# A fused attention and mixer kernel: what its planner counts of the DMA queue, when a batch's first sum is turned, and where the last 64 keys' scores come from

## The chip, the cores and the metric

The kernel runs on one core of one Trainium2 chip. The metric is device time in microseconds (us) of one execution. Of the kernel before there are three timed executions and one profiled execution. TensorE (PE) does the matmuls, VectorE (DVE) and ScalarE (ACT) the elementwise work, GpSimd (POOL) a few casts at the start, and SyncE (SP) issues every DMA, one after the other, in the order in which the program has them.

## The reference

There are 8 batches; a sequence has S = 3136 rows, D = 256, the attention's inner size is 64, the mixer's rank is 32 and its hidden size is 1024.

```
scores = z @ z.T / S                    # (3136, 3136), symmetric
attn   = max(scores, 0) ** 2
x      = u * (attn @ v)                 # (3136, 256)
h      = x.T @ U @ V                    # rank 32, along the sequence
u2     = x + h.T
out    = u2 + max(u2 @ w_ch1, 0) @ w_ch2
```

All inputs and the output are float32 in memory. The kernel casts to bfloat16 for the matmuls and accumulates in float32. S is 24 full tiles of 128 rows and a tail of 64 rows.

## The kernel before

**Tiling.** A batch's rows form groups: six of 512 rows (g = 0 to 5, four tiles each) and one of 64 rows (g = 6). An "item" is one pair (batch b, group g); the main loop runs over the 56 items in order and emits the matmuls of an item's attention times v ("AV"), interleaved with scores that later items need and with mixer work of items that lie a batch back. Nearly all matmuls use 64 of the 128 rows of the array and go in pairs, one pair member on each half of the rows (`pair`, L159); so line L164 is the line of nearly every matmul.

**Scores.** The scores of a batch are made by key block J and query group g into "blocks" (128 x 4 x 512 bf16, L383): matmuls of 512 columns into PSUM, `rectify` (L317) out of PSUM by ACT or DVE, `square` (L313) by DVE. Scores are symmetric. Most blocks with J > g are therefore made once, and the block for (b, J, g) is the transpose of the block for (b, g, J): `issue_turn` (L336) takes a free block and issues a transposing DMA on SP. There are 20 blocks; `take_block` and `give_block` pass them around.

**The last 64 keys.** The tail's keys against the 512 queries of a group are a job called "last", one for each two groups, three a batch (`jobs_of`, L906; L355 and L378): a pair of matmuls of 512 columns, a rectify and a square into `last_sb`. `av_end` (L599) reads it as the last step of a group's AV. The tail's 64 queries against all keys are made apart by `score_small` (L416) into `attn_small`, which is read by `av_small` (L552), the AV of group 6. By symmetry `attn_small` holds the same numbers as the "last" scores, turned.

**The mixer.** `t1_all` (L630) makes x.T @ U for a whole batch once all seven groups have x. `u2_unit` (L661) makes h for a group by matmuls, DVE adds x to it (L708, `out_sb`, float32), `cast` (L181) makes the bf16 copy into `x_bf` on whichever of ACT and DVE the planner holds to be free sooner, and `x_turn` (L621) turns that copy by a DMA into `u2T`. `ch1_part` (L753) multiplies w_ch1 with `u2T`, so its first matmul of a group has to wait for that DMA; `ch2_stream` (L795) does w_ch2, and `ch2_out` (L823) adds and stores.

**What sets the order.** The program is emitted by a planner in Python that keeps a clock in its own units (L96, one unit is a matmul pair of 256 columns: `pe`, L121) and three estimates in `free_at`: when ACT, DVE and the SP queue will be free. `book` (L102) adds a cost to one of them, `hold` (L106) defers an action to a time, and `run_held` (L109) does what is due after each emitted piece. A block that is squared becomes ready to be turned (`ready_turns`); `run_held` issues one when the estimate for SP says that the queue is free (L118), each turn being booked at 34 units (L345). Loads, stores and the turns of z and x are not booked. If AV comes to a block that has not been turned, `lhs` in `av_stream` (L509) issues the turn at that place. `emit` (L857) merges three queues of work into the stream of AV and ch2 matmuls by places that are written out in the main loop. Engines and the DMA queue each run their own instructions in program order; waits between them are semaphores.

Of the kernel before, what the change touches and what calls it, by code (L numbers as in the profile page):

```python
# [9 lines left out]
BF16 = mybir.dt.bfloat16  # L10
# [8 lines left out]
def kernel(  # L19
# [17 lines left out]
    P = 128  # L37
# [60 lines left out]
    held = []  # L98
    unturned = {}
    ready_turns = []  # L100

    def book(eng, ready, cost):  # L102
        free_at[eng] = max(free_at[eng], ready) + cost
        return free_at[eng]

    def hold(due, f):  # L106
        held.append((due, len(held), f))

    def run_held(now=None):  # L109
        now = clock[0] if now is None else now  # L110
        while True:
            ripe = [h for h in held if h[0] <= now]
            if not ripe:
                break
            h = min(ripe, key=lambda e: (e[0], e[1]))
            held.remove(h)
            h[2]()
        while ready_turns and free_at["sp"] <= now:  # L118
            issue_turn(min(ready_turns, key=lambda e: (e[0], e[2], e[1])))

    def pe(cost):  # L121
# [75 lines left out]
    def load_tail(raw, c0, a, n):  # L197

        for h in range(2):
            nc.sync.dma_start(out=raw[h * TAIL : (h + 1) * TAIL, c0 : c0 + n], in_=a[NF * P : S, :])  # L200


    def load_z_piece(b, t0, n, raw, tail=True):
        m = min(n, NF - t0)
        nc.sync.dma_start(  # L205
            out=raw[:, : m * dqk].rearrange("p (t d) -> p t d", d=dqk), in_=rows_of(z[b])[:, t0 : t0 + m, :]
        )
        if n > m and tail:
            load_tail(raw, m * dqk, z[b], dqk)
            load_tail(raw, n * dqk, v[b], D)  # L210
# [15 lines left out]
    def load_v_piece(b, k, raw):  # L226
        nc.sync.dma_start(
            out=raw.rearrange("p (t d) -> p t d", d=D), in_=rows_of(v[b])[:, k * GT : (k + 1) * GT, :]
        )

    def v_copy(b, k, raw, copy):
        copy(out=v_bfs[b][:, k * GT : (k + 1) * GT, :], in_=raw.rearrange("p (t d) -> p t d", d=D))
# [41 lines left out]
    def load_u(b, g):  # L274
        g0, gw = groups[g]
        t = pool.tile([P, GT, D], FP32, name="u_sb", bufs=2)
        if gw >= P:
            nc.sync.dma_start(
                out=t[:, : gw // P, :],
                in_=rows_of(u[b])[:, g0 // P : (g0 + gw) // P, :],  # L280
            )
        else:
            nc.sync.dma_start(out=t[:gw, 0, :], in_=u[b, g0 : g0 + gw, :])
        u_sbs[b, g] = t


    def z_turn_dma(b):
        nc.sync.dma_start_transpose(
            out=zzTs[b], in_=z_bfs[b].rearrange("p t c d -> p (t c d)")
        )  # L290

    def z_turn(b, t0, copy):
        n = min(2 * GT, NT - t0)
# [55 lines left out]
    def score_pairs(jobs):  # L349

        made = []
        for b, g, job in jobs:
# [23 lines left out]
                GW,  # L376
            )
            if job == "last":  # L378
                lasts[b, g // 2] = pool.tile([P, 2, GW], BF16, name="last_sb")
                made.append((lasts[b, g // 2], k, ps, None, None))  # L380
                continue
            if h == 0:
# [30 lines left out]
        score_finish(score_pairs(jobs))  # L413


    def score_small(b, g):  # L416
        zzT = zzTs[b]
        g0, gw = groups[g]
# [5 lines left out]
        for p0 in range(0, npair, per):  # L424
            n = min(per, npair - p0)
            pk, ps = take_ps()
            for k in range(n):
                pair(
                    pk,
                    [  # L430
                        (
                            jj,
                            jj,
                            dict(
                                out=ps[:, jj, k * gw : (k + 1) * gw],
                                lhsT=half(zzT, jj, (2 * (p0 + k) + jj) * P, P),
                                rhs=half(zzT, jj, g0, gw),
                                start=(k == 0),
                                stop=(k == n - 1 and (jj == 1 or p0 + n < npair)),
                            ),  # L440
                        )
                        for jj in range(2)
                    ],
                    gw,
                )
            made.append((p0, n, pk, ps))
# [105 lines left out]
    def av_small(b, g):  # L552
# [3 lines left out]
        for jt in range(NT):  # L556
            c = jt % 2
            for h in range(2):
                nc.tensor.matmul(  # L559
                    out=ps[c * hp : c * hp + rows, h, :D],  # L560
                    lhsT=smalls[b][h * hp : (h + 1) * hp, jt, :],
                    rhs=v_bfs[b][h * hp : (h + 1) * hp, jt, :],
                    start=(jt < 2),
                    stop=(jt >= NT - 2),
                    tile_position=(h * hp, c * hp),
                )
# [31 lines left out]

    def av_end(b, g, box):  # L599

        last = lasts[b, g // 2]
        for a in range(2):
            pair(
                box["k"],
# [2 lines left out]
                    a,  # L607
                    lambda h, q: dict(
                        out=four(box["ps"])[:, q, :],
                        lhsT=last[h, g % 2, q * P : (q + 1) * P],  # L610
                        rhs=v_bfs[b][h, NF, :],
                        start=False,
                        stop=(a == 1),
# [7 lines left out]
    def x_turn(b, g, turned):  # L621
# [3 lines left out]
            out=turned[:, :n, :, :rows].rearrange("p q d c -> p (q d) c"),  # L625
            in_=xs[b, g][:rows, :n, :].rearrange("p q d -> p (q d)"),
        )


    def t1_all(b):  # L630
# [30 lines left out]
    def u2_unit(b, g, turn=True):  # L661
# [161 lines left out]
    def ch2_out(b, g, acc):  # L823
# [6 lines left out]
        nc.vector.tensor_tensor(out=o, in0=acc, in1=o, op=ALU.add)  # L830
        dst = rows_of(out[b])[:, t0 : t0 + n, :] if rows == P else out[b, t0 * P : S, None, :]
        nc.sync.dma_start(out=dst, in_=o)
        if (b, g) in o_blocks:
            give_block(o_blocks.pop((b, g)))

# [80 lines left out]
    def load_U():  # L916
        entry, raw = stage_block()
        nc.sync.dma_start(out=raw[:, : NF * R].rearrange("p (t r) -> p t r", r=R), in_=rows_of(moe_U))
        nc.sync.dma_start(out=raw[:TAIL, NF * R : NT * R], in_=moe_U[NF * P :, :])

        def casts():
            cast(U_bf[:, :NF, :], raw[:, : NF * R].rearrange("p (t r) -> p t r", r=R), NF * R)
# [5 lines left out]
    def load_w(k):  # L928
        def step(i):
# [4 lines left out]
            else:  # L934
# [2 lines left out]
                    in_=moe_w_ch2.rearrange("(t p) d -> p t d", p=P)[:, i * GT : (i + 1) * GT, :],  # L937
                )
                dst = w2_bf[:, i * GT : (i + 1) * GT, :].rearrange("p t d -> p (t d)")

            def casts(entry=entry, raw=raw, dst=dst):
                cast(dst, raw, GT * D)
# [7 lines left out]
    def load_V(i0):  # L950
        n = P // 4

        def step(i):
            entry, raw = stage_block()
            w = n * NF + (S - NF * P if i == 3 else 0)
            for c in range(NREP):
                nc.sync.dma_start(out=raw[c * R : (c + 1) * R, :w], in_=moe_V[:, i * n * NF : i * n * NF + w])

            def casts(i=i, entry=entry, raw=raw):
                cast(  # L960
# [102 lines left out]
    for b in range(B):  # L1063
        for g in range(NQ):
# [18 lines left out]
    for t in range(n_items):  # L1083
# [169 lines left out]
```

## Time and profile before

| what | us |
|---|---|
| three timed executions | 1010.28, 1007.97, 1010.57 |
| their median | 1010.28 |
| the profiled execution's own time | 1010.08 |
| its span, from the first to the last instruction | 1008.3 |
| TensorE matmul busy in the span | 986.7 (98%) |
| VectorE busy | 653.6 (65%) |
| ScalarE busy | 520.2 (52%) |
| DMA queue q1, share of the 16 DMA engines' span | 76.3% |

The span is cut by engine: a busy time is the time in which the engine ran at least one instruction. TensorE matmuls overlap in pairs, so the mean duration of one matmul is longer than the time by which it pushes the next. The profile's row of granted clock says what share of TensorE's full speed the chip gave it in a slice. A wait in the profile has the form "who waited <- for whom: total, times, longest"; a row of the timeline has start, duration, engine, line, operation, output<-input, count, and in brackets the idle time before it with what ended it. SPq rows are DMA issues on SP: their duration is the time that the queue was occupied with the issue, and the data lands later.

### The profile page before, as it was taken

How to read it: one execution, taken by the hardware profiler on the slowest of the kernel's cores; microseconds unless marked ns; L12 is line 12 of the kernel's file. 1: busy time of each engine (PE TensorE's matmuls, PEld its weight loads, DVE VectorE, ACT ScalarE, POOL GpSimd, SP SyncE). 2: the span in 40 equal slices, each digit the busy share in tenths (PEclk: the TensorE clock that was granted, in tenths of full speed). 3: DMA queues.
4: the chain of work that ended last, by engine and by line, in shares of the span. 5: the costliest groups of instructions: out<-in, count | busy, mean ns of one | idle time of the engine just before them, and what ended most of it. 6: DMA issues, size and time to landing. Idle time of an engine off the chain costs nothing.

```text
span 1008.3 us, 35337 instructions
## 1 busy us (share of the span) xinstructions
PE 986.7 (98%) x16179; PEld 784.7 (78%) x16179; DVE 653.6 (65%) x820; ACT 520.2 (52%) x599; POOL 17.2 (2%) x24
## 2 busy tenths in 40 slices
PE   6999899999999999999999999999999999999997
PEld 3898688877787777778777877778777777787776
DVE  5986675668666685666756677566776667653453
ACT  6896653357524573355733456444653356522453
POOL 4100000000000000000000000000000000000000
PEclk9999899999999999999999999999999999999999
DMA  7997998478966799568995789846798577873142
GB/s 247 187 257 178 235 170 166 130 166 186 213 142 165 152 199 218 149 145 181 182 209 157 129 193 188 210 127 140 179 216 185 137 158 143 160 127 88 45 103 94
DMA packets 337061, 167.84 MB, mean 166 GB/s; under 512 B 312336, under 2 KB 315408, under 8 KB 336912
## 3 DMA queue, kind: packets, MB, share of 16 engines
q1 hardware_dynamic: 336912, 165.59, 76.3%
q8 instruction: 126, 2.06, 0.8%
q14 instruction: 23, 0.19, 0.1%
HBM read 62.56 MB, written 25.69 MB: 88 GB/s over the span
## 4 chain that ended last, share of the span: by engine, by line
PE 94%; DVE 2%; ACT 2%; DMA 1%; issue 0%; POOL 0%; SPq 0%; POOLq 0%; ACTq 0%
PE ps L164 92%; PE ps L559 1%; DVE blk L315 1%; ACT blk L793 1%; PE ps L635 1%; DMA blk<-in_v_dram 1%; ACT blk L325 1%; PE ps L843 0%; DMA u2T<-x_bf 0%; DMA stage<-in_v_dram 0%; POOL z_bf L213 0%; SPq L205 0%; DVE blk L321 0%; DVE out_sb L708 0%; DVE blk L830 0%
## 5 line engine op out<-in xcount | busy, mean ns | idle before, releaser
L164 PEld LDWEIGHTS <-blk 64*128 64x128 bf16 x12288 | 617.6, 94 | 153.6 <-POOLq L154 8.7
L164 PE MATMUL ps<-v_bf,blk 64*128 64x256 bf16 x9216 | 617.2, 270 | 2.3 <-DVE blk L315 1.8
L325 ACT ACTIVATE blk<-ps 128x1024 bf16<-128x1024 f32 x324 | 323.4, 1027 | 337.2 <-PE ps L164 334.0
L315 DVE TENSOR_TENSOR blk<-blk 128x1024 bf16<-128x1024 bf16 x352 | 237.7, 701 | 34.1 <-ACT blk L325 33.4
L164 PE MATMUL ps<-u2T,w_bf 64*128 64x512 bf16 (+1 forms) x1792 | 239.1, 351 | 4.3 <-DMA u2T<-x_bf 3.5
L164 PE MATMUL ps<-w_bf,blk 64*128 64x256 bf16 x3072 | 193.7, 269 | 0.2
L790 DVE TENSOR_SCALAR blk<-ps 128x1024 bf16<-128x1024 f32 x96 | 115.7, 1205 | 102.3 <-PE ps L164 102.3
L793 ACT ACTIVATE blk<-ps 128x1024 bf16<-128x1024 f32 (+1 forms) x128 | 107.3, 847 | 82.4 <-PE ps L164 74.1
L164 PE MATMUL ps<-zzT 64*128 64x512 bf16 (+1 forms) x944 | 143.5, 342 | 1.9 <-ACT zzT L305 1.7
L164 PEld LDWEIGHTS <-w_bf 64*128 64x128 bf16 x1792 | 91.6, 94 | 35.1 <-DMA u2T<-x_bf 3.8
L592 DVE TENSOR_TENSOR x_bf<-ps,u_sb 128x1024 bf16<-128x1024 f32 x48 | 58.8, 1224 | 63.0 <-PE ps L164 62.9
L708 DVE TENSOR_TENSOR out_sb<-ps,x_bf 128x1024 f32<-128x1024 f32 (+1 forms) x49 | 54.3, 1107 | 53.7 <-PE ps L164 53.6
L830 DVE TENSOR_TENSOR out_sb<-ps,out_sb 128x1024 f32<-128x1024 f32 x42 | 51.3, 1222 | 18.3 <-PE ps L164 18.3
L164 PEld LDWEIGHTS <-zzT 64*128 64x128 bf16 x944 | 43.9, 95 | 9.2 <-ACT zzT L305 2.2
L325 ACT ACTIVATE last_sb<-ps 128x1024 bf16<-128x1024 f32 x23 | 23.5, 1024 | 26.5 <-PE ps L164 26.5
L321 DVE TENSOR_SCALAR blk<-ps 128x1024 bf16<-128x1024 f32 x24 | 29.4, 1224 | 10.3 <-PE ps L164 8.7
L186 DVE CAST x_bf<-out_sb 128x1024 bf16<-128x1024 f32 x33 | 22.8, 690 | 0.5
L186 DVE CAST v_bf<-stage 128x1024 bf16<-128x1024 f32 (+1 forms) x34 | 21.2, 626 | 0.0
L164 PE MATMUL ps<-t_sb,V_bf 64*128 64x256 bf16 x200 | 20.8, 269 | 0.0
L164 PE MATMUL ps<-v_bf,last_sb 64*128 64x256 bf16 x192 | 18.6, 269 | 0.0
L830 DVE TENSOR_TENSOR blk<-ps,blk 128x1024 f32<-128x1024 f32 x6 | 7.3, 1225 | 16.0 <-PE ps L164 15.9
L578 ACT COPY u_sb<-ps 64x512 f32<-64x512 f32 x8 | 4.7, 582 | 23.9 <-PE ps L559 23.9
(67 smaller groups left out, 249.5 us busy)
## 6 DMA issues: line engine op xcount, KB each, us to landing
u_sb<-in_u_dram SPq DMA_DIRECT2D x48, 512.0 KB, 5.0
stage<-in_v_dram SPq DMA_DIRECT2D x42, 512.0 KB, 6.0
out_dram<-out_sb SPq DMA_DIRECT2D x42, 512.0 KB, 3.1
stage<-in_z_dram SPq DMA_DIRECT2D x7, 512.0 KB, 5.5
blk<-in_v_dram SPq DMA_DIRECT2D x6, 512.0 KB, 7.2
out_dram<-blk SPq DMA_DIRECT2D x6, 512.0 KB, 2.6
blk<-in_moe_w_ch_dram SPq DMA_DIRECT2D x4, 512.0 KB, 5.8
stage<-in_z_dram SPq DMA_DIRECT2D x7, 256.0 KB, 5.7
```

Of the source, the lines that this page charges most:

```text
L164: ins = nc.tensor.matmul(**args)
L186: nc.vector.tensor_copy(out=out, in_=in_)
L315: nc.vector.tensor_tensor(out=a, in0=a, in1=a, op=ALU.mult)
L321: nc.vector.tensor_scalar(out=dst, in0=src, scalar1=scale, scalar2=0.0, op0=ALU.mult, op1=ALU.max)
L325: nc.scalar.activation(out=dst, in_=src, func=AF.Relu, scale=scale)
L559: nc.tensor.matmul(out=ps[c * hp : c * hp + rows, h, :D], lhsT=smalls[b][h * hp : (h + 1) * hp, jt, :], rhs=v_bfs[b][h * hp : (h + 1) * hp ...
L592: nc.vector.tensor_tensor(out=xs[b, g][:rows, :n, :], in0=four(box["ps"])[:rows, :n, :], in1=u_sbs[b, g][:rows, :n, :], op=ALU.mult,)
L635: nc.tensor.matmul(out=pt[c * R : (c + 1) * R, 0, :D], lhsT=U_bf[:rows, it, :], rhs=xs[b, g][:rows, q, :], start=(it < NREP), stop=(it + N ...
L708: nc.vector.tensor_tensor(out=o[:rows, :n, :], in0=four(ps)[:rows, :n, :], in1=x, op=ALU.add)
L790: nc.vector.tensor_single_scalar(out=r, in_=ps[:, :, :gw], scalar=0.0, op=ALU.max)
L793: nc.scalar.activation(out=r, in_=ps[:, :, :gw], func=AF.Relu)
L830: nc.vector.tensor_tensor(out=o, in0=acc, in1=o, op=ALU.add)
```

## The change

The change has three parts.

First, a new helper `queued` books the SP estimate for every transfer: plain ones by their size, turning ones (z and x) at about twice that rate. `run_held` therefore holds the turns of score blocks back for as long as the estimate says that loads and stores occupy the queue.

Second, for a batch's first group (g = 0) `u2_unit` is placed earlier in its item (place 22 in place of 34), its bf16 copy is emitted on DVE right behind the add, its `x_turn` is held until six units before the copy's booked end, and while it is pending (`urgent`) no turn of a score block is issued by `run_held`.

Third, for batches 1 to 7 there are no "last" jobs. `last_turn` turns the first 24 tiles of `attn_small` (1536 columns, 12 tiles of 128 columns) with one transposing DMA into `last_sb`, at the start of the batch's first item. For that `score_small` of the next batch is emitted in item g = 5 of the batch before it (batch 0's own in item g = 4), the tiles of `attn_small` are kept in a swapped order (`place_of`), and `last_sb` has one buffer in place of two, so that batch 0's "last" jobs for g = 2 and g = 4 move one item later.

```diff
+    urgent = []
...
+    def queued(kb, turned=False):
+
+        book("sp", clock[0], kb * (17 / 256 if turned else 15 / 512))
...
-        while ready_turns and free_at["sp"] <= now:
+        while ready_turns and free_at["sp"] <= now and not urgent:
             issue_turn(min(ready_turns, key=lambda e: (e[0], e[2], e[1])))
...
         for h in range(2):
             nc.sync.dma_start(out=raw[h * TAIL : (h + 1) * TAIL, c0 : c0 + n], in_=a[NF * P : S, :])
+            queued(n / 4)
...
             out=zzTs[b], in_=z_bfs[b].rearrange("p t c d -> p (t c d)")
         )
+        queued(NT * P / 4, True)
...
             if job == "last":
-                lasts[b, g // 2] = pool.tile([P, 2, GW], BF16, name="last_sb")
+                flat = last_tile().rearrange("p n c -> p (n c)")
+                lasts[b, g // 2] = flat[:, : 2 * GW].rearrange("p (a c) -> p a c", c=GW)
...
+    def place_of(jt):
+
+        if jt == NF:
+            return jt
+        return jt // GT * GT + (0, 2, 1, 3)[jt % GT]
+
+    def last_tile():
+        return pool.tile([P, NF // 2, P], BF16, name="last_sb", bufs=1)
+
+    def last_turn(b):
+
+        lasts[b] = last_tile()
+        nc.sync.dma_start_transpose(
+            out=lasts[b], in_=smalls[b][:, :NF, :].rearrange("p t c -> p (t c)")
+        )
+        book("sp", clock[0], 26)
...
-        last = lasts[b, g // 2]
+        def last(h, q):
+            if b:
+                return lasts[b][h, 2 * g + q % 2, :]
+            return lasts[b, g // 2][h, g % 2, q * P : (q + 1) * P]
...
             x_turn(b, g, u2Ts[b, g])
+            urgent.clear()
...
-        hold(done - 3, down)
+        if g == 0:
+            urgent.append((b, g))
+            nc.vector.tensor_copy(out=x, in_=o[:rows, :n, :])
+            hold(book("dve", done, 6.3) - 6, turned)
+        else:
+            hold(done - 3, down)
...
-        if g % 2 == 0:
+        if g % 2 == 0 and b == 0:
             j.append((b, g, "last"))
...
+            elif b == 0 and g and g % 2 == 0:
+                todo[t] += new[:-1]
+                todo[t + 1] += new[-1:]
...
+        if g_now == 0 and t:
+            last_turn(att[0])
...
-        if av and g_now == NQ - 1:
-            qm.append((55, 2, False, lambda: score_small(att[0], NQ)))
+        if av and t == NQ - 2:
+            qm.append((55, 2, False, lambda: score_small(0, NQ)))
+        if av and g_now == NQ - 1 and b_next < B:
+            qm.append((55, 2, False, lambda: score_small(b_next, NQ)))
...
-            qm.append((34 if u2i[1] == 0 else 40, 1, False, lambda: u2_unit(*u2i)))
+            qm.append((22 if u2i[1] == 0 else 40, 1, False, lambda: u2_unit(*u2i)))
```

More of the change, by code (lines that the diff above doesn't have):

```diff
@@ L207, in load_z_piece @@
         )
+        queued(m * dqk / 2)
         if n > m and tail:
@@ L229, in load_v_piece @@
         )
+        queued(GT * D / 2)
     def v_copy(b, k, raw, copy):
@@ L283, in load_u @@
             nc.sync.dma_start(out=t[:gw, 0, :], in_=u[b, g0 : g0 + gw, :])
+        queued(gw)
         u_sbs[b, g] = t
@@ L435, in score_small @@
                                 out=ps[:, jj, k * gw : (k + 1) * gw],
-                                lhsT=half(zzT, jj, (2 * (p0 + k) + jj) * P, P),
+                                lhsT=half(zzT, jj, place_of(2 * (p0 + k) + jj) * P, P),
                                 rhs=half(zzT, jj, g0, gw),
@@ L560, in av_small @@
                     out=ps[c * hp : c * hp + rows, h, :D],
-                    lhsT=smalls[b][h * hp : (h + 1) * hp, jt, :],
+                    lhsT=smalls[b][h * hp : (h + 1) * hp, place_of(jt), :],
                     rhs=v_bfs[b][h * hp : (h + 1) * hp, jt, :],
@@ L609, in av_end @@
                         out=four(box["ps"])[:, q, :],
-                        lhsT=last[h, g % 2, q * P : (q + 1) * P],
+                        lhsT=last(h, q),
                         rhs=v_bfs[b][h, NF, :],
@@ L627, in x_turn @@
         )
+        queued(n * D / 4, True)
     def t1_all(b):
@@ L832, in ch2_out @@
         nc.sync.dma_start(out=dst, in_=o)
+        queued(n * rows)
         if (b, g) in o_blocks:
@@ L919, in load_U @@
         nc.sync.dma_start(out=raw[:TAIL, NF * R : NT * R], in_=moe_U[NF * P :, :])
+        queued(NF * R / 2)
         def casts():
@@ L939, in step @@
                 dst = w2_bf[:, i * GT : (i + 1) * GT, :].rearrange("p t d -> p (t d)")
+            queued(GT * D / 2)
             def casts(entry=entry, raw=raw, dst=dst):
@@ L957, in step @@
                 nc.sync.dma_start(out=raw[c * R : (c + 1) * R, :w], in_=moe_V[:, i * n * NF : i * n * NF + w])
+                queued(w / 8)
             def casts(i=i, entry=entry, raw=raw):
```

## The prediction

> **What bounds the kernel now.** I read the page first, then the stretches by batch, then who TensorE waited for, then the timeline at the places that these named.
>
> ```profile
> span 1008.3 us, 35337 instructions
> ...
> PE 986.7 (98%) x16179; PEld 784.7 (78%) x16179; DVE 653.6 (65%) x820; ACT 520.2 (52%) x599; POOL 17.2 (2%) x24
> ...
> PEclk9999899999999999999999999999999999999999
> ...
> PE 94%; DVE 2%; ACT 2%; DMA 1%; issue 0%; POOL 0%; SPq 0%; POOLq 0%; ACTq 0%
> ```
>
> TensorE is busy for 98% of the span and carries 94% of the chain that ended last. So a matmul taken away shortens the time, and work taken from DVE or ACT does so only where TensorE stands still for it. Table of stretches (start:end, length, busy time of each engine with count, then granted clock, DMA share, GB/s):
>
> ```profile
> core 0: us, PE busy (x) PEld busy (x) DVE busy (x) ACT busy (x) POOL busy (x), PEclk, DMA share, GB/s
> 92.25:118.34 26.09, 22.07 (x398) 17.80 (x393) 18.33 (x28) 17.00 (x22) 0.00 (x0) 0.98 1.10 220
> ...
> 114.84:118.38 3.54, 0.00 (x1) 0.00 (x0) 1.42 (x2) 0.00 (x0) 0.00 (x0) 0.88 1.23 168
> 118.34:130.40 12.06, 11.78 (x131) 7.53 (x132) 6.11 (x8) 7.45 (x9) 0.00 (x0) 0.75 1.02 203
> 330.42:452.08 121.66, 121.57 (x2019) 95.69 (x2017) 81.24 (x103) 60.87 (x72) 0.00 (x0) 1.00 0.83 173
> 452.08:573.74 121.66, 121.57 (x2019) 95.62 (x2017) 81.22 (x103) 60.87 (x72) 0.00 (x0) 1.00 0.88 173
> 938.72:1008.30 69.58, 63.91 (x998) 48.60 (x993) 33.71 (x40) 30.42 (x38) 0.00 (x0) 1.00 0.30 84
> ```
>
> A middle batch takes 121.66 us with TensorE busy for 121.57 of it: there only matmuls can be saved. One place differs: 3.54 us without a matmul, and behind it 12.06 us at 0.75 of the clock, the one dip in the row PEclk. What was waited for:
>
> ```profile
> PE ps L164 <- DMA u2T<-x_bf: 3.5, 1, 3.5
> ```
>
> ```profile
> 105.05 0.38 PE L164 MATMUL ps<-t_sb,V_bf 64*128 64x256 bf16 x4
> ...
> 105.47 1.22 DVE L708 TENSOR_TENSOR out_sb<-ps,x_bf 128x1024 f32<-128x1024 f32 x1
> 106.61 1.28 DVE L315 TENSOR_TENSOR blk<-blk 128x1024 bf16<-128x1024 bf16 x2
> ...
> 107.81 0.69 DVE L186 CAST x_bf<-out_sb 128x1024 bf16<-128x1024 f32 x1
> ...
> 109.22 4.64 SPq L341 DMA_TRANSPOSE blk<-blk  x1
> ...
> 113.96 1.25 SPq L624 DMA_TRANSPOSE u2T<-x_bf  x1
> ...
> 114.22 0.62 PE L164 MATMUL ps<-v_bf,blk 64*128 64x256 bf16 x8
> ...
> 118.38 1.04 PE L164 MATMUL ps<-u2T,w_bf 64*128 64x512 bf16 x4 [3.54 <-DMA u2T<-x_bf]
> ```
>
> The first mixer group's x + h is in bf16 at 108.5, but SP spends 109.22 to 113.86 on the turn of a score block; only then is x turned, and it lands 4.4 us later, at the matmul's start. This place costs 3.54 us of standing and 12.06 x (1 - 0.75) = 3.0 us of clock: 6.5 us.
>
> The sums below start from the profiled execution's own 1010.08 us (its span plus 1.8 us around it), 0.2 under the median 1010.28. About 0.3%, 3 us, is what a measurement of this kernel can tell from no change.
>
> **The change, part by part.**
>
> **1. The "last" scores of batches 1 to 7 go: 21 jobs.** Each is a pair of matmuls of 512 columns, an eviction and a square.
>
> ```profile
> 332.19 0.40 PE L164 MATMUL ps<-zzT 64*128 64x512 bf16 x2
> ...
> 332.41 1.39 PE L164 MATMUL ps<-v_bf,blk 64*128 64x256 bf16 x22
> ```
>
> ```profile
> L325 ACT ACTIVATE last_sb<-ps 128x1024 bf16<-128x1024 f32 x23 | 23.5, 1024 | 26.5 <-PE ps L164 26.5
> L315 DVE TENSOR_TENSOR last_sb<-last_sb 128x1024 bf16<-128x1024 bf16 x24 | 16.4, 683 | 0.2 <-ACT last_sb L325 0.2
> ```
>
> Such a pair moves the next matmul by 332.41 - 332.19 = 0.22 us; 21 of them are 4.6 us, all on TensorE's path: -4.6. The evictions (21 x 1.02 us on ACT) and squares (21 x 0.68 us on DVE) lie beside the matmuls, and cost nothing to lose except at one place of each batch, item g = 6, where the last job of the next batch's g = 0 stands among w_ch1 matmuls:
>
> ```profile
> 341.51 1.02 ACT L793 ACTIVATE blk<-ps 128x1024 bf16<-128x1024 f32 x1
> ...
> 342.09 0.40 PE L164 MATMUL ps<-zzT 64*128 64x512 bf16 x2
> ...
> 342.54 1.02 ACT L325 ACTIVATE last_sb<-ps 128x1024 bf16<-128x1024 f32 x1
> ```
>
> By the spacing above a matmul should follow that pair at 342.31; the next one starts when the eviction by L793 has ended, at 342.58, so TensorE loses 0.27 us. In the changed order the same w_ch1 matmuls take PSUM tiles that were emptied earlier. Six batches have this pattern: between 0 (another eviction is as late) and -1.6; I take -1.6, as the two tiles in question are asked for over 1 us after their evictions can start.
>
> **2. last_turn: 7 transposing DMAs, of 12 tiles each.** No row shows one. The turns around it do:
>
> ```profile
> blk<-blk SPq DMA_TRANSPOSE x112, 5.2
> u2T<-x_bf SPq DMA_TRANSPOSE x55, 3.3
> ```
>
> A block turn has 16 tiles, an x turn 8, so about 4.2 us from issue to landing and some 2 us of the queue. The first reader is `av_end` of group 0, some 15 us of matmuls later: 0. It has TensorE's last reads of the single `last_sb` buffer to wait for, which lie an item back. What stands behind it on SP is z's load for the next batch (read 16 us later) and the first x_turn, see 4. `score_small` is as often there as before, one batch earlier: 0. `place_of` only permutes: 0.
>
> **3. The first x + h sooner (batch 0's mixer, the wait at 114.84).** In the changed order `u2_unit` stands 1.0 us of matmul columns earlier, the copy follows the add with no squares between (0 in place of 1.2 us), and on SP the block turn of 109.22 is behind it; in front are last_turn, z's loads and two loads of u, all but the first of which had gone out before 109.22 in the kernel before. So: add about 104.5 to 106, copy to about 107, turn issued by then, landed within 4.4 us, 111.4. The reader comes at about 114.5. Wait and dip go: -6.5. What is late next here is nothing that I can find; 3 us of cover remain. If they were used up by the DMA engines, which are full in this stretch (share 1.10 over 92.25 to 118.34), the -6.5 shrinks to 0 (rival two).
>
> **4. Loads and stores are booked: block turns are held back.** This moves DMAs, and adds none. In batches 0 and 1, where the weights are loaded too, the estimate for SP now runs ahead of the planner's clock for long, and turns wait until AV needs them. I counted in both programs how much matmul work stands between what a DMA waits for and its first reader. For block turns the least was 27 us of columns; now it is 19, with one exception of 4.0. That is batch 1, the turn of the block for g = 4, J = 5, needed by AV of group 5. AV found it not turned and issued it at the place of use, so it stands on SP right behind an x_turn that has only just become possible:
>
> ```
> L351 DmaTransposeAnt blk19_3981<-blk9_3864
> L656 DmaTransposeAnt u2T_4046<-x_bf_1650
> L351 DmaTransposeAnt blk0_4058<-blk10_3230      # the late one
> ```
>
> The first two stand in the same order in the kernel before, and TensorE's matmuls there are the same too (16 of AV, 2 scores, 4 of w_ch1, 14 of AV, the small scores, 16 of AV, 4 of w_ch1, 2 of AV, then the reader), so the rows of before give the times:
>
> ```profile
> 203.69 6.28 SPq L341 DMA_TRANSPOSE blk<-blk  x2
> ...
> 205.71 0.40 PE L164 MATMUL ps<-t_sb,V_bf 64*128 64x256 bf16 x4
> ...
> 207.89 0.69 DVE L186 CAST x_bf<-out_sb 128x1024 bf16<-128x1024 f32 x1
> ...
> 209.89 0.82 PE L164 MATMUL ps<-v_bf,blk 64*128 64x256 bf16 x12
> 210.05 1.69 SPq L624 DMA_TRANSPOSE u2T<-x_bf  x1
> ```
>
> ```profile
> blk<-blk SPq DMA_TRANSPOSE x3, 4.4
> ```
>
> SP is free of the x_turn at 210.05 + 1.69 = 211.74, the block's turn goes out at 211.75, and lands 4.4 us later (the median of the three between 195 and 220 us): 216.1. The reader would start two matmuls into the row at 209.89, at 210.0. TensorE stands still for 6.1 us, between 5.7 (the x_turn occupies SP for 1.25 us, as in the row at 113.96) and 7.0 (landing in 5.2, the median of all block turns). Nothing else can run meanwhile: TensorE's queue is in order, and behind the reader are all the rest of AV, scores and mixer. A wait of 3.54 us was followed by a dip that cost 3.0 us; I take 3.0 for this longer one too, between 0 (no dip) and 3.0. Together +9.1, between +5.7 and +10.0.
>
> [...]
>
> In the middle batches the x_turns come no later relative to their readers: in the changed order the first group's has 9.2 us of columns (7.1 before), the third's stands ahead of the block turn that it followed, and the others are within 0.5. 0, and small gains are not to be had where TensorE is busy throughout.
>
> **5. The end.** The tail (938.72 on, TensorE idle for 5.7 us of 69.58) has the same order but for names: 0.
>
> **Sum:** 1010.08 - 4.6 - 1.6 - 6.5 + 9.1 = 1006.5 us.
>
> **The rivals.**
>
> One: the block's turn is not late, because SP runs ahead of what I think. Against it: the x_turn in front of it needs the copy that ends at 208.58 and occupies SP for 1.25 us at least, and with 4.4 us to landing the data cannot be there before 214.2, against 210.0. For it: only that I read the order of a program and not a run. 1010.08 - 4.6 - 1.6 - 6.5 = 997.4 us.
>
> Two, the slower side: the first x_turn is late all the same, with last_turn in the place of the block turn. The place is SP at 100 to 107 us; for it speak the DMA share of 1.10 there, and that a block turn in that stretch occupied the queue for 4.64 us. It decides if the turn of x lands later than about 114.5, that is, goes out after 110. If last_turn only takes the place of the block turn, the 6.5 us stay, 1013.0; if it comes on top of the same loads and the turn of x goes out 1 us later than the 113.96 of before, 4.5 + 3.0 us are lost here: 1006.5 + 7.5 = 1014.0, the price I give it.
>
> Three: the booking changes nothing that matters and last_turn's load on the DMA engines (share 0.83 in a middle batch) makes x_turns late in each batch. Price from the dip and a wait of 1 us: 6 batches x 1 us and two dips, 1006.5 + 12 = 1018. Against it: 12 tiles come to some 315 a batch (15 block turns of 16, six x turns of 8, the turn of z of 25), 4%.
>
> **How the numbers follow.** Forecast 0.66, rival one 0.15, rival two 0.12, rival three 0.07. The forecast's own range is 1003 to 1009 (the ends of the wait, the dip and of part 1). For 8 in 10 the range reaches from rival one, 997, up to 1012.5, short of rival two as priced; what is left out is rivals two and three. Faster by over 0.3% means under 1007.2: six tenths of the forecast's cases and all of rival one, 0.55. Within 0.3%: the rest of the forecast and some of rival two, 0.31. Slower: 0.14.
>
> **What would show it.** Right: TensorE's waits have no x_turn at 115 us, and have one wait for a block's turn of about 6 us near 200 us; PEclk dips there and not at 118; a middle batch takes 120.7 us in place of 121.66; zzT matmuls of 512 columns are 42 fewer; seven new turns of 12 tiles land in about 4 us. Wrong: no wait near 200 us (then 997), a wait at 115 us (then 1013), waits that come back in each batch (then 1018), or a middle batch still at 121.66.

## The result and the profile after

The changed kernel takes 1005.4 us (median of 5 runs, 1003.74 to 1007.66); the kernel before, run beside it, 1010.57 us (1007.97 to 1011.47). The ratio is 0.9956, with a 95% interval of 0.9937 to 0.9976: 0.44% faster, 1.1 us under the forecast of 1006.5 and inside its range. The profiled execution took 1006.67 us, with a span of 1004.8.

From the page of the changed kernel, its span, busy times and granted clock in 40 slices:

```profile
span 1004.8 us, 35249 instructions
...
PE 980.5 (98%) x16137; PEld 781.4 (78%) x16137; DVE 635.6 (63%) x793; ACT 505.9 (50%) x584; POOL 17.2 (2%) x24
...
PEclk9999999989999999999999999999999999999999
```

There are 42 matmuls fewer, and the one dip of the clock (6.83 us at 0.50 of full speed: 207.44 to 214.27, before 117.52 to 124.35) has moved from the fifth slice to the ninth. What TensorE waited for (total, times, longest):

```profile
PE ps L169 <- DMA blk<-blk: 6.1, 1, 6.1
...
PE ps L169 <- ACT v_bf L189: 1.8, 1, 1.8
```

The wait for the first x + h (u2T, 3.5 us before) is gone, and one of 6.1 us for a block's turn is there. The wait for v was 0.5 us before, and ended by VectorE:

```profile
PE ps L164 <- DVE v_bf L186: 0.5, 1, 0.5
```

Stretches, with columns as in the table of before:

```profile
204.56:210.62 6.06, 0.00 (x1) 0.01 (x2) 0.99 (x1) 0.60 (x3) 0.00 (x0) 0.74 1.00 184
...
203.13:331.85 128.72, 122.66 (x2015) 94.58 (x2011) 78.74 (x98) 59.20 (x70) 0.00 (x0) 0.97 0.81 171
331.85:452.58 120.73, 120.73 (x2015) 95.42 (x2011) 78.75 (x98) 59.20 (x70) 0.00 (x0) 1.00 0.84 178
```

A middle batch takes 120.73 us, where it took 121.66. The late turn in the timeline, SP's queue and its reader:

```profile
202.43 1.69 SPq L351 DMA_TRANSPOSE blk<-blk  x1
...
204.21 1.91 SPq L656 DMA_TRANSPOSE u2T<-x_bf  x1
...
206.18 2.23 SPq L351 DMA_TRANSPOSE blk<-blk  x1
...
210.62 0.61 PE L169 MATMUL ps<-v_bf,blk 64*128 64x256 bf16 x4 [6.06 <-DMA blk<-blk]
```

The first x + h of batch 0's mixer and, behind it, the new wait for v:

```profile
106.75 0.69 DVE L756 CAST x_bf<-out_sb 128x1024 bf16<-128x1024 f32 x1
107.47 1.25 SPq L656 DMA_TRANSPOSE u2T<-x_bf  x1
...
109.86 1.05 ACT L189 CAST w_bf<-blk 128x1024 bf16<-128x1024 f32 x1
...
111.70 1.05 ACT L189 CAST v_bf<-stage 128x1024 bf16<-128x1024 f32 x1
...
112.81 0.39 PE L169 MATMUL ps<-v_bf,blk 64*128 64x256 bf16 x4 [1.77 <-ACT v_bf L189]
```

The x + h is on the queue at 107.47 (113.96 before). The cast of batch 1's last block of v, which VectorE made at 110.22 before, is now given to ScalarE, in order behind evictions and the cast of a weight.

**One stretch to compare all kernels by.** Run times move by some 4 us within one kernel. Part of that is probably the start: the matmul that follows TensorE's second wait for a square stands at 31.87 to 34.68 us in the thirteen profiles here, behind the same matmuls; TensorE's wait there for z_bf on GpSimd is 0 to 4.0 us long. So I also compare the stretch from that matmul to the one behind TensorE's last wait, for L883's input (L843 in the kernel before). Before:

```profile
33.71:961.91 928.20, 922.72 (x15263) 737.03 (x15264) 610.23 (x771) 476.76 (x552) 4.84 (x5) 1.00 0.79 167
```

and after:

```profile
34.15:958.37 924.22, 915.73 (x15222) 733.39 (x15223) 592.57 (x744) 462.30 (x537) 4.83 (x5) 1.00 0.82 171
```

928.20 - 924.22 = 4.0 us less.

### The profile page after: what moved, and what is told of

It reads as the page before. It is cut to its first block, busy times and chain, and to the rows that moved or that the text cites. A ratio compares the mean times of both kernels' runs of the same rounds, so it can differ in the third digit from the quotient of the medians.

```text
span 1004.8 us, 35249 instructions
## 1 busy us (share of the span) xinstructions
PE 980.5 (98%) x16137; PEld 781.4 (78%) x16137; DVE 635.6 (63%) x793; ACT 505.9 (50%) x584; POOL 17.2 (2%) x24
## 4 chain that ended last, share of the span: by engine, by line
PE 95%; DMA 1%; ACT 1%; DVE 1%; issue 1%; SPq 0%; POOL 0%; POOLq 0%; ACTq 0%
PE ps L169 92%; PE ps L587 1%; PE ps L668 1%; ACT blk L335 1%; DMA blk<-in_v_dram 1%; DVE blk L325 1%; PE ps L883 0%; DMA blk<-blk 0%; ACT blk L832 0%; DMA blk<-in_moe_V_dram 0%; POOL z_bf L220 0%; SPq L656 0%; DVE blk L331 0%; DVE blk L869 0%; DVE x_bf L620 0%
## 5 line engine op out<-in xcount | busy, mean ns | idle before, releaser
L335 ACT ACTIVATE blk<-ps 128x1024 bf16<-128x1024 f32 x334 | 334.0, 1027 | 371.7 <-PE ps L169 368.5
L829 DVE TENSOR_SCALAR blk<-ps 128x1024 bf16<-128x1024 f32 (+1 forms) x111 | 128.4, 1157 | 104.7 <-PE ps L169 103.9
L832 ACT ACTIVATE blk<-ps 128x1024 bf16<-128x1024 f32 (+1 forms) x113 | 96.4, 863 | 87.1 <-PE ps L169 85.6
L169 PE MATMUL ps<-zzT 64*128 64x512 bf16 (+1 forms) x902 | 135.2, 340 | 1.7 <-ACT zzT L315 1.7
L169 PEld LDWEIGHTS <-zzT 64*128 64x128 bf16 x902 | 41.7, 95 | 7.4 <-ACT zzT L315 2.2
L331 DVE TENSOR_SCALAR blk<-ps 128x1024 bf16<-128x1024 f32 x14 | 17.1, 1225 | 13.7 <-PE ps L169 12.8
L191 DVE CAST v_bf<-stage 128x1024 bf16<-128x1024 f32 x28 | 19.1, 684 | 0.0
L191 DVE CAST x_bf<-out_sb 128x1024 bf16<-128x1024 f32 x26 | 17.9, 689 | 0.2
L189 ACT CAST v_bf<-stage 128x1024 bf16<-128x1024 f32 (+1 forms) x20 | 17.1, 855 | 0.0
L608 DVE TENSOR_TENSOR u_sb<-ps,u_sb 64x512 f32<-64x512 f32 x8 | 5.5, 683 | 17.1 <-ACT u_sb L606 17.1
```

What stands on the lines that cost most here:

```text
L169: ins = nc.tensor.matmul(**args)
L189: nc.scalar.copy(out=out, in_=in_)
L191: nc.vector.tensor_copy(out=out, in_=in_)
L331: nc.vector.tensor_scalar(out=dst, in0=src, scalar1=scale, scalar2=0.0, op0=ALU.mult, op1=ALU.max)
L335: nc.scalar.activation(out=dst, in_=src, func=AF.Relu, scale=scale)
L829: nc.vector.tensor_single_scalar(out=r, in_=ps[:, :, :gw], scalar=0.0, op=ALU.max)
```

## The experiments

The three parts of the change are: **counting** (loads and stores are booked in SP's estimate), **sooner** (first u2 at place 22, copy straight on VectorE, its turn ahead of block turns), and **turned** (the last 64 keys' scores of batches 1 to 7 turned by DMA). The theory behind the first runs: the three parts act as the prediction says, and the late turn comes of the counting alone. All kernels in one table; the stretch is that of one profile each, the ratio that of the runs to the kernel before on the same chip.

| kernel | counting | sooner | turned | stretch, us | time, us | ratio, 95% interval |
|---|---|---|---|---|---|---|
| before | | | | 928.20 | 1008.8 to 1010.57 | 1 |
| e_bookonly | x | | | 922.10 | 1004.41 | 0.9949 (0.9937 to 0.9962) |
| e_firstonly | | x | | 925.05 | 1005.78 | 0.9979 (0.9964 to 0.9993) |
| e_lastonly | | | x | 928.31 | 1008.38 | 0.9997 (0.9985 to 1.0009) |
| e_bookfirst | x | x | | 922.37 | 1003.59 | 0.9939 (0.9925 to 0.9953) |
| e_nofirst | x | | x | 928.85 | 1010.11 | 1.0011 (0.9992 to 1.0031) |
| e_nobook | | x | x | 919.23 | 1000.90 | 0.9922 (0.9906 to 0.9939) |
| after | x | x | x | 924.22 | 1005.40 | 0.9956 (0.9937 to 0.9976) |
| e_due | x | x | x | 916.19 | 998.41 | 0.9901 (0.9886 to 0.9916) |
| e_no26 | x | x | x | 916.22 | 996.44 | 0.9876 (0.9862 to 0.9889) |
| e_vcast | x | x | x | 914.27 | 995.46 | 0.9871 (0.9852 to 0.9889) |
| e_fill | x | x | x | 923.48 | 1004.84 | 0.9960 (0.9945 to 0.9975) |
| e_twice | x | x | x | 936.50 | 1018.31 | 1.0095 (1.0070 to 1.0119) |

### The late turn: its order (e_due)

```diff
-            issue_turn(min(ready_turns, key=lambda e: (e[0], e[2], e[1])))
+            issue_turn(min(ready_turns, key=lambda e: (e[2], e[0], e[1])))
```

> Changed kernel, but the ready block turns are issued in the order in which their readers come (batch, reading group, then source group; before: reading group first, whatever the batch). Theory (the 6.1 us wait comes of the order in which the planner sends turns that are all ready): batch 1's turn for group 5 goes out two turns sooner, the 6.1 us wait and the 1.8 us of half-rate clock behind it are gone, every other stretch stays; 1005.4 - 7.9 = 997.5 us, and the 1.8 us wait for batch 1's v stays. Rival (the DMA queue is overfull there, some turn has to be late): another turn or an x + h is waited for instead, for 3 us or more, and the time stays within 3 us of 1005.4.

Measured: 998.41 us; the 6.1 us wait and the dip are gone, the 1.8 us wait for v is left. The stretch:

```profile
34.02:950.21 916.19, 913.78 (x15221) 734.57 (x15222) 592.48 (x744) 462.27 (x537) 4.83 (x5) 1.00 0.83 173
```

The stretch is 924.22 - 916.19 = 8.0 us shorter, against 7.9 expected: 6.06 of wait and 1.8 of clock. The rival falls: the queue has room for this turn. In the changed kernel the planner sorts ready turns by the reading group first; batch 2's turns for groups 1, 2 and 3 went out ahead of batch 1's for group 5, although that one is read first. (So the turn is three places sooner here, not two as expected.)

### Is it the counting? (e_nobook, e_bookfirst, e_bookonly, e_no26)

```diff
     def queued(kb, turned=False):
 
-        book("sp", clock[0], kb * (17 / 256 if turned else 15 / 512))
+        return
```

> Changed kernel, with the new counting of loads and stores in the DMA queue's estimate left out; the first x + h sooner and the turned last keys stay. Theory (the counting alone made the turn late, and the first x + h's own place, copy and precedence are enough against the first wait): no wait of 6.1 us near 200 us, none for the first x + h near 110 us, 1005.4 - 7.9 = 997.5 us. Rival (the counting is what keeps block turns out of the first x + h's way): the late turn is gone but a wait of some 3.5 us for the first x + h with its 3 us of half-rate clock is back, 1005.4 - 7.9 + 6.5 = 1004 us.

Measured: 1000.90 us. No late turn, as both expected; for the first x + h no wait either, so the rival falls: beside the turned keys, the sooner place clears the x + h's way without the counting. But it is 3.0 us behind e_due in the stretch, 2.2 of it through waits that neither named:

```profile
132.66 1.49 PE L169 MATMUL ps<-w_bf,blk 64*128 64x256 bf16 x24 [1.51 <-ACT blk L335]
134.52 0.61 PE L169 MATMUL ps<-w_bf,blk 64*128 64x256 bf16 x8 [0.38 <-DVE blk L829]
157.83 0.61 PE L169 MATMUL ps<-u2T,w_bf 64*128 64x512 bf16 x4 [0.26 <-DMA u2T<-x_bf]
```

The first of them has a ScalarE behind it that itself stood for a block buffer:

```profile
131.58 1.94 ACT L335 ACTIVATE blk<-ps 128x1024 bf16<-128x1024 f32 x2 [3.74 <-DMA blk<-blk]
```

Just ahead of it three block turns in a row occupy the queue for 11.1 us, from 119.77 (two, for 7.8 us, in e_due): where nothing holds block turns back they bunch up, and a buffer comes free late.

The next kernels are the changed one without its third part (e_bookfirst), and without the second part too (e_bookonly). For the third part taken out, the core is

```diff
-        if g % 2 == 0 and b == 0:
+        if g % 2 == 0:
             j.append((b, g, "last"))
...
-        if g_now == 0 and t:
-            last_turn(att[0])
```

and e_no26 leaves one booking out:

```diff
         nc.sync.dma_start_transpose(
             out=lasts[b], in_=smalls[b][:, :NF, :].rearrange("p t c -> p (t c)")
         )
-        book("sp", clock[0], 26)
```

> The first two parts without the third: loads and stores counted, first x + h sooner; the last keys' scores made by TensorE as in the kernel before. Theory (batch 1's turn comes late only where the counting and the 26 units booked for the turned last keys come together): no 6.1 us wait near 200 us, and none for the first x + h, since no block turn stands in the queue within 4 us of it: the time of the kernel before less 6.5 us. Rival (the counting alone makes the turn late): the 6.1 us wait is there, the time of the kernel before and 1.4 us more.

> The first part alone: loads and stores counted. Theory (the counting moves no turn away from right ahead of the first x + h where the third part is missing): a wait of 2 to 3.5 us for the first x + h with half-rate clock behind it stays, no 6.1 us wait: the time of the kernel before, within 3 us. Rival (the counting clears the first x + h's way by itself, as it does beside the third part): no wait for it, the time of the kernel before less 6.5 us.

> Changed kernel without the 26 units that the turn of the last keys books in the queue's estimate; the turn itself is issued as before. Theory (the turn of batch 1 is late because the estimate, not the queue, is full): no 6.1 us wait, about the time of the kernel with the turns in their readers' order, 998.4 us (997 to 1000). Rival (what the estimate books is really in the queue, and a turn issued sooner only holds up another transfer): waits of 3 us or more elsewhere, 1002 us or more.

e_bookfirst met its theory: no late turn with the counting in, a ratio of 0.9939, 5.8 us off the stretch. So the counting alone does not make the turn late, against what e_nobook's theory had said. e_no26 shows the other half: with the 26 units gone and all else kept, the turn is in time and the stretch is 916.22, the same as with the turns in their readers' order. What makes the turn late is a full estimate, not a full queue: it takes both the counting and those 26 units, and the sort by reading group.

e_bookonly missed its theory, and its rival was nearly right. The block turn stands in the queue right ahead of the first x + h, as the theory had it, and the wait is 0.30 us all the same:

```profile
108.26 1.88 SPq L351 DMA_TRANSPOSE blk<-blk  x1
110.23 1.78 SPq L653 DMA_TRANSPOSE u2T<-x_bf  x1
```

```profile
115.49 0.60 PE L169 MATMUL ps<-u2T,w_bf 64*128 64x512 bf16 x4 [0.30 <-DMA u2T<-x_bf]
```

In the kernel before, a turn issued at 105.26 and another at 109.22, which sat 4.64 us on the queue, stood there. Here there is one, for 1.88 us, and the x + h is out 3.7 us sooner without having been made sooner.

### The second part alone (e_firstonly) and left out (e_nofirst)

The core of the second part; the place 22 and the use of `urgent` belong to it, as in the diff of the change.

```diff
-        hold(done - 3, down)
+        if g == 0:
+            urgent.append((b, g))
+            nc.vector.tensor_copy(out=x, in_=o[:rows, :n, :])
+            hold(book("dve", done, 6.3) - 6, turned)
+        else:
+            hold(done - 3, down)
```

> Only the second part of the change: a batch's first u2 at place 22 in place of 34, its copy straight on VectorE, its turn ahead of ready block turns; estimate and last keys as in the kernel before. Theory: the 3.54 us wait for the first x + h and the 3.0 us of half-rate clock behind it go and nothing else changes: 1010.4 - 6.5 = 1003.9 us. Rival (block turns already in the queue hold the x + h as before, since only those not yet issued are kept back): 2 us or more of the wait stay, with a clock dip, 1008 us or more.

> Changed kernel without its second part: the first u2 of a batch at place 34 again, its copy by the old path, its turn not ahead of block turns; counting and turned last keys stay. Theory (the counting alone clears the queue around the first x + h; the second part then buys only margin): no wait for the first x + h near 115 us, the 6.1 us wait near 200 us as in the changed kernel, and waits of 0.3 to 2 us in some of batches 2 to 6, where the margin of 0.9 to 1.9 us is used up by the 2 us later place: 1006.5 us (1005.4 to 1008). Rival (the second part is what removed the first wait): 2 us or more of wait near 115 us with half-rate clock behind it, 1009 us or more.

Alone, it leaves most of the wait, so the rival was nearer in that, though not in the dip and the time that it named; the ratio is 0.9979. The x + h is issued at 110.34, 3.6 us sooner than before, but takes long to land, with block turns issued at 106.03 and 111.68 around it:

```profile
u2T<-x_bf SPq DMA_TRANSPOSE x1, 7.6
```

```profile
115.48:117.99 2.51, 0.01 (x1) 0.00 (x1) 1.43 (x2) 0.00 (x0) 0.00 (x0) 1.00 1.28 117
```

In the changed kernel no block turn is near it, and it lands 4.5 us after its issue. The clock is 1.00 throughout here: this wait of 2.51 us set off no dip. On the stretch 3.15 us are gained, where a wait 1.0 us shorter and no half-rate clock would give 4.0; the 0.9 us between I did not find.

Left out, beside the other two: no wait for the first x + h, as the theory said; but 4.6 us are lost on the stretch against the changed kernel, where 1.1 us were expected, most of it by waits of 0.75 and 2.36 us in the first mixer groups of two later batches and 1.7 us of half-rate clock behind the longer one. The second of these, queue and reader:

```profile
719.84 2.16 SPq L439 DMA_TRANSPOSE last_sb<-attn_small  x1
722.11 4.30 SPq L351 DMA_TRANSPOSE blk<-blk  x1
726.51 1.26 SPq L656 DMA_TRANSPOSE u2T<-x_bf  x1
...
731.06 0.61 PE L169 MATMUL ps<-u2T,w_bf 64*128 64x512 bf16 x4 [2.36 <-DMA u2T<-x_bf]
```

last_turn has taken 2.2 us of the queue and a block turn 4.3, ahead of the x + h. So the second part is needed for the later batches (two of them here), because the third one fills the queue there.

### The third part alone (e_lastonly)

The changed kernel with the edits of e_nobook, and those of the second part undone.

> Only the third part of the change: the last 64 keys' scores of batches 1 to 7 turned by DMA, small group first; estimate and first x + h as in the kernel before. Theory (from the two traces: -0.93 us in each of six batches, -1.3 at the end, +0.8 in the start and some +1.3 by the wait for batch 1's v, which belongs to this part): about 1010.4 - 4.9 = 1005.5 us, with the 3.5 us wait for the first x + h still there and no 6.1 us wait. Rival (the v wait belongs to the counting or to the sooner x + h): 1010.4 - 6.8 = 1003.6 us and no wait for batch 1's v beyond the 0.5 us of before.

Nothing gained: ratio 0.9997, where the theory had 4.9 us and the rival 6.8; both missed. The rows of TensorE's waits:

```profile
PE ps L169 <- DMA u2T<-x_bf: 8.8, 5, 5.4
...
PE ps L169 <- ACT v_bf L189: 1.4, 1, 1.4
```

What is saved in matmuls goes into five waits for a batch's first x + h, the largest 5.36 us where it was 3.54: last_turn (at 103.09) and two block turns (4.90 us from 109.61, 3.56 us from 115.23) stand ahead of it, and it goes out at 118.88. This is what rival two of the prediction described; the small waits in some later batches are like rival three, which had them in each. With this part alone both came true in kind. The wait for v belongs to this part: 1.4 us here and 1.8 in e_nobook, while e_firstonly, e_bookfirst and e_bookonly have the 0.5 of before.

### The wait for v (e_vcast)

```diff
-            hold(clock[0] + (90 if g_now == NQ else 15 if t > NG else 45) + 12 * i, f)
+            hold(clock[0] + (74 if t == NQ else 90 if g_now == NQ else 15 if t > NG else 45) + 12 * i, f)
```

made in e_due.

> The kernel with block turns in the order of their readers, and the cast of batch 1's last block of v due 16 planner units sooner, which puts it on VectorE between two squares in place of ScalarE behind two evictions. Theory (the 1.77 us wait for v is a wait of TensorE that nothing else covers): 998.4 - 1.8 = 996.6 us, no wait for v near 111 us. Rival (TensorE, 1.8 us ahead, meets the first x + h or a block turn that is not there yet): a new wait of 1 us or more, 997.5 us or more.

Measured: 995.46 us, no wait for v, and no new one in the batches; the stretch is 916.19 - 914.27 = 1.9 us shorter. The rest of the 2.9 us between the medians lies outside the stretch, 1.2 us of it in the start (34.02 against 32.78). This kernel has the lowest time here, 1.29% faster than before (0.9871, 0.9852 to 0.9889) and ahead of the changed one; e_no26, which lacks this edit, lies within that interval.

### The clock behind the wait (e_fill)

```diff
                 if (g, jb, b) in ready_turns:
                     issue_turn((g, jb, b))
+                    fill(b, 24)
...
+    def fill(b, n):
...
+        for _ in range(n):
+            pair(
...
+                            lhsT=half(zzTs[b], jj, 0, P),
+                            rhs=half(zzTs[b], jj, 0, GW),
...
```

> Changed kernel with 48 matmuls of 64x512 on zzT, whose results nobody reads, put on TensorE ahead of the AV matmul that waits for the late turn (some 5.2 us of work inside the 6.1 us wait). Theory (what the wait costs beyond its own length is the half-rate clock after an idle TensorE, and the 4 us between the runs of one kernel come of where the clock's 3.41 us windows lie against the wait): the rest of the wait is about 0.9 us, no half-rate stretch near 207 us, about 998.4 + 6 = 1004.4 us with all runs within 1 us. Rival (the clock or the spread have another cause): half-rate stretch and a spread of 3 us or more as before, 1005.4 us.

```profile
202.36 5.36 PE L169 MATMUL ps<-zzT 64*128 64x512 bf16 x48
209.43 0.72 PE L169 MATMUL ps<-v_bf,blk 64*128 64x256 bf16 x10 [1.72 <-DMA blk<-blk]
```

```profile
209.43:213.11 3.68, 3.68 (x60) 2.91 (x62) 0.85 (x1) 2.05 (x2) 0.00 (x0) 1.00 0.00 0
```

The same 3.68 us behind the wait ran at 0.50 in the changed kernel (34 matmuls in place of these 60). From the wait's end to the end of the stretch the changed kernel needs 958.37 - 210.62 = 747.75 us, this one 955.40 - 209.43 = 745.97: 1.8 us, the cost of the dip. The expected 0.9 us of leftover wait came out as 1.72: x + h and block turn took 5.7 and 5.4 us to land in place of 4.0 and 4.4, for a reason that stays open. So the gain on the stretch is 0.7 us, which the run times (1004.84 against 1005.4) cannot tell from nothing. The theory's 3.41 us is half of the 6.83 us at half rate in the changed kernel (207.44 to 214.27); e_nofirst has a stretch of 3.41 us (732.14 to 735.55). The second half of the theory falls: the runs still spread from 1002.67 to 1006.46.

### The cover of the turned keys (e_twice)

```diff
         nc.sync.dma_start_transpose(
             out=lasts[b], in_=smalls[b][:, :NF, :].rearrange("p t c -> p (t c)")
         )
+        nc.sync.dma_start_transpose(
+            out=lasts[b], in_=smalls[b][:, :NF, :].rearrange("p t c -> p (t c)")
+        )
```

> Changed kernel with the turn of the last keys issued twice in each of batches 1 to 7, the second into the same tile. Theory (the turn's own cover is the 1.6 to 2.8 us that the trace of the changed kernel shows between landing and reader in batches 2 to 6, and the first x + h behind it has 0.9 to 1.9 us): the second copy takes 1.5 to 2.7 us of the queue and lands some 3 to 5 us later, so TensorE waits 1 to 3 us in about five batches, some with half-rate clock behind: 1005.4 + 5 to 15 us. Rival (about 15 us of cover, as the prediction had it): no new wait, 1005.4 us within 3.

Measured: 1018.31 us, 9.5 over the kernel before, and 12.3 us over the changed kernel on the stretch. TensorE now waits for the turned keys:

```profile
PE ps L169 <- DMA last_sb<-attn_small: 5.9, 5, 1.8
...
PE ps L169 <- DMA u2T<-x_bf: 1.7, 3, 0.7
```

```profile
359.71 2.10 SPq L439 DMA_TRANSPOSE last_sb<-attn_small  x1
365.63 1.42 SPq L442 DMA_TRANSPOSE last_sb<-attn_small  x1
367.15 1.61 SPq L659 DMA_TRANSPOSE u2T<-x_bf  x1
```

The rival, 15 us of cover, falls. The push was rougher than planned: the second copy, which writes the same tile, is issued 5.9 us after the first, and all of SP stands behind it. 7.6 us of the 12.3 are these waits. The clock accounts for some 2.8 more: a new half-rate piece of 3.41 us at 738.04 costs 1.7, and the dip behind the late turn has 2.48 + 3.42 us of work at half rate, 1.1 us more than the changed kernel's. The last 1.9 us I did not find.

## Why the prediction was right, and where not

The sum came out within 1.1 us, partly by luck, because errors cancelled: part 1 saved 1.3 us more and the dip cost 1.2 us less than forecast, while a wait for v that the sum does not have took 1.3 us and the first wait gave 0.4 to 0.7 us less. By its own steps:

- **Step 1, the "last" jobs: right in kind, somewhat undersized.** A middle batch was to take 120.7 us and takes 120.73; 42 matmuls are gone. The third part is worth 922.37 - 916.19 = 6.2 us between e_bookfirst and e_due, and that has 1.3 us of additional wait for v in it: 7.5 us without, against 6.2 forecast (the two differ in the order of turns too). About half of the 1.3 us more lies in the last batch: from the same w_ch1 matmuls near its start to the end of the stretch it takes 142.87 us (from 815.50) in place of 144.17 (from 817.74), 1.3 us less, where three jobs of 0.22 us were counted. The rest I did not find.
- **Step 2, last_turn at 0: right for this kernel, with a cover far too large.** No matmul of the changed kernel waits for it. But it was estimated to land in 4.2 us, with "some 15 us" before its reader:

```profile
last_sb<-attn_small SPq DMA_TRANSPOSE x7, 5.9
```

```profile
357.80 2.11 SPq L439 DMA_TRANSPOSE last_sb<-attn_small  x1
360.01 1.28 SPq L656 DMA_TRANSPOSE u2T<-x_bf  x1
...
365.33 0.38 PE L169 MATMUL ps<-v_bf,last_sb 64*128 64x256 bf16 x4
...
365.98 0.59 PE L169 MATMUL ps<-u2T,w_bf 64*128 64x512 bf16 x4
```

  It lands 5.9 us after 357.80, at 363.7, 1.6 us before its reader; the x + h behind it lands 5.1 us after 360.01, 0.9 us before its own. e_twice, e_lastonly and e_nofirst show what happens when these margins are gone. What I missed is the place in the queue: it goes out behind the next batch's z loads, late in the item.
- **Step 3, the first x + h: the effect right, the cause only half.** The wait and its dip go, 5.8 us (e_bookfirst) to 6.1 (e_bookonly), against 6.5. The prediction gave this to the sooner place. That is enough beside the turned keys (e_nobook has no wait there), but not against the kernel before (e_firstonly, 2.51 us are left); the counting, which the prediction did not credit, is enough in both (e_nofirst has no wait there, e_bookonly 0.30 us). "What is late next here is nothing that I can find" failed: the cast of v is late, 1.77 us in place of 0.5, through the third part.
- **Step 4, the late turn: found, and its wait exact** (6.1 us, on the turn of batch 1 for g = 4, J = 5). Two things in it were off. The dip behind it was taken at 3.0 us and cost 1.8: half of the half-rate time, 3.18 of 6.83 us, fell into the wait. And its cause was not the booking of loads and stores alone, but that together with last_turn's 26 units and the sort by reading group. That the x + h of middle batches come no later was right, by the second part: without it two of them do come late.
- **Step 5, the end at 0** held but for the last batch's share of step 1.

Rival one, no late turn at 997.4 us, is what e_due (998.41) and e_no26 (996.44) measure: its price was right, its condition not met.

## What to carry to other kernels

Correcting a planner's estimate of a queue lets it hold work back, so the order among what is held must then be the order of need; here one sort key was worth 8 us, more than the change itself. Parts of a change that share a queue did not add up here: alone the turned keys gained nothing (0.9997) and with the counting but not the sooner x + h they lost (1.0011, the late turn included), and beside both, with the block turns in their readers' order, they are worth 6 us. A cost of 0 for a transfer should come with its margin, counted from where it really stands in the queue to its reader.

## What was not expected of the hardware

Behind a wait the half-rate clock lasted 6.83 us (before, 117.52 to 124.35; the changed kernel, 207.44 to 214.27) or 3.41 us (e_nofirst, 732.14 to 735.55), and the length of a wait did not tell whether any followed. Three cuts in pieces of 3.41 us, columns as above; the changed kernel:

```profile
204.03:207.44 3.41, 0.53 (x6) 0.10 (x2) 0.99 (x1) 1.13 (x5) 0.00 (x0) 1.00 1.12 204
207.44:210.85 3.41, 0.23 (x4) 0.17 (x6) 0.00 (x0) 0.00 (x0) 0.00 (x0) 0.50 0.83 157
210.85:214.27 3.42, 3.42 (x34) 2.23 (x32) 0.00 (x0) 1.02 (x1) 0.00 (x0) 0.50 0.00 0
```

the kernel before:

```profile
114.11:117.52 3.41, 0.73 (x14) 0.45 (x9) 1.82 (x2) 0.09 (x1) 0.00 (x0) 1.00 1.24 168
117.52:120.94 3.42, 2.56 (x20) 1.39 (x22) 0.00 (x0) 0.00 (x0) 0.00 (x0) 0.50 1.07 223
120.94:124.35 3.41, 3.41 (x30) 2.00 (x28) 0.41 (x1) 3.22 (x4) 0.00 (x0) 0.50 1.00 292
```

and e_nofirst:

```profile
728.73:732.14 3.41, 1.08 (x16) 0.79 (x18) 2.00 (x3) 0.37 (x1) 0.00 (x0) 1.00 1.16 179
732.14:735.55 3.41, 3.41 (x28) 1.80 (x26) 1.00 (x1) 2.11 (x3) 0.00 (x0) 0.50 0.82 221
```

The full-rate pieces ahead of the half-rate ones have 0.53, 0.73 and 1.08 us of TensorE's work here. In the kernel before, a half-rate piece with 2.56 of 3.42 us of work was followed by another; those with 3.42 us (the changed kernel) and 3.41 us (before, e_nofirst) were followed by full rate. At 0.50 of the clock half of the work in a piece is lost: 1.8 us after, (2.56 + 3.41) / 2 = 3.0 before, 1.7 in e_nofirst.

A wait of 2.51 us in e_firstonly lost none, although it is longer than e_nofirst's 2.36. Where the pieces end may be why; this is an estimate from the drops of the clock. In the changed kernel they are at 207.44 and, at the end, at 1002.75: 795.31 us apart, 233 times 3.4133. The clock of e_firstonly drops once, at the end of the trace, at 1003.87; 260 pieces of 3.4133 us back from there is 116.40, inside the wait (115.48 to 117.99):

```profile
112.99:116.40 3.41, 2.50 (x46) 2.21 (x42) 2.37 (x4) 1.85 (x2) 0.00 (x0) 1.00 1.46 258
116.40:119.81 3.41, 1.82 (x28) 1.35 (x30) 0.51 (x1) 0.41 (x1) 0.00 (x0) 1.00 0.90 185
...
1003.87:1005.90 2.03, 0.00 (x0) 0.00 (x0) 0.00 (x0) 0.00 (x0) 0.00 (x0) 0.50 0.25 99
```

Cut so, the wait lies in two pieces, with 2.50 and 1.82 us of work, and the clock stays at 1.00 behind both. Cut in this way from 20 to 999 us, the traces of before and of the changed kernel have no other full-rate piece with less than 2.47 us of work, and no other drop. The work in a piece alone does not part the cases here: one with 1.57 us was followed by half rate (e_twice, 734.62 to 738.04), one with 1.53 us was not (e_lastonly, 730.88 to 734.29).
